# Longer rows in the expert table, first rows zeroed from a batch's own tile, and a new order of work

## The chip, the cores and the metric

The kernel runs on one NeuronCore of a Trainium2 chip. A core has five engines that work through their own instruction streams, each strictly in its written order: TensorE (PE, matrix multiplications; loads of its stationary operand are shown as PEld), VectorE (DVE), ScalarE (ACT), GpSimd (POOL), and SyncE (SP), which here only issues DMAs. They wait for each other, and for DMAs, by semaphores. The metric is the device time of one execution in microseconds. Before the change, three runs took 211.22, 211.44 and 217.73 us; their median is 211.44.

## The reference: what is computed

Two blocks follow each other. The first is an attention with sketched features and no softmax, for 4 batches of 4 heads with 1088 positions of 32 values; the second routes each of the 4352 resulting rows of 128 values to one of 8 experts.

```python
def phi(x):                                   # 8 x 8 products of two sketches
    a = np.einsum('rd,bhsd->bhsr', S1, x)
    b = np.einsum('rd,bhsd->bhsr', S2, x)
    return np.einsum('bhsi,bhsj->bhsij', a, b).reshape(*x.shape[:-1], r * r)
q_p, k_p = (phi(q), phi(k))
kv = np.einsum('bhsf,bhsd->bhfd', k_p, v)
z = np.sum(k_p, axis=2)
num = np.einsum('bhsf,bhfd->bhsd', q_p, kv)
den = np.einsum('bhsf,bhf->bhs', q_p, z)[..., None] + 1e-06
x = (num / den).transpose(0, 2, 1, 3).reshape(B * S, H * D)

logits = x @ w_gate
expert_idx = np.argmax(logits, axis=1)
gate_w = softmax(logits)[np.arange(N), expert_idx]
for e in range(E):
    mask = expert_idx == e
    out[mask] = gate_w[mask, None] * (np.maximum(x[mask] @ w1[e], 0.0) @ w2[e])
```

## The kernel before, in words

The work is cut into named steps, and the string `ORDER` (lines 20 to 49) is the order in which they are recorded. Recording a step appends its instructions to the streams of the engines that it uses; there is no scheduler behind it. So a step that stands early in `ORDER` also stands early in every engine's stream, and whatever waits there holds up all that the same engine has behind it.

**Attention.** `S.t` and `S.m` prepare the sketch matrix; after `S.m` the function `late_constants` (line 287) is called, which builds two constants with copies on GpSimd, `sel` (line 290) and `heads` (line 293). Keys and queries come in chunks of 512 positions: `k21` are the keys of batch 2, chunk 1, `q21` its queries; `kr0` and `kr1` are the 64 positions that are left over of two batches each, `qr0` and `qr1` likewise. Of a chunk, `.t` transposes on PE, `.x` copies to SBUF on ACT, `.a` multiplies by the sketches on PE, `.l`, `.s` and `.o` (ACT, DVE, DVE) form the 64 products, and `.v` of a key chunk sums keys times values on PE. When a batch's keys are done, its steps `e0` to `e3` finish the sums: `.r` adds the remainder, `.k` copies (ACT), `.t` (lines 454 and 460) multiplies by `heads` and `sel` on PE, and `.c`, `.m`, `.z` store the result. Only then can that batch's queries be multiplied (`.n` and `.N`), divided (`.p`, `.e`) and written into `x_rows` (`.y`) and the gate sums (`.g`).

**Routing.** For batch `b`, `rb.a` to `rb.d` choose each row's expert and its place in a table in device memory, `xs_dram`, with 4352 rows for each of 8 experts and one further stretch of the same length. `rb.p` is the part on PE. Then `rb.s0`, `rb.s1` and so on scatter 128 rows each with an indirect DMA from GpSimd (line 641), with `RESTS[b]` small memsets behind each (`breathe`, line 564). A row has `XW` = 130 words: 128 values, the gate weight, and the row's number. The numbers are written into `x_rows` by iotas on GpSimd at the start. Before any row is scattered, the first 128 rows of each of the nine stretches are filled with zeros and a number that is no row's, `ABSENT`, by one DMA on SyncE's queue (line 981); scatters wait for it, since they write the same table.

**Experts.** `t0` to `t2` compute which expert and which rows belong to each tile of 128 rows. Tiles 0 to 9 use rows of batches 0 and 1 alone, later ones those of later batches. Of tile `j7`, `.l` loads the rows (SyncE), `.x` transposes (PE, line 846), `.c` copies, `.w` fetches the first weight (DVE), `.u` and `.U` are the first product (PE, line 863), `.r` and `.q` the rectifier, `.d` the second product (PE, line 898), `.y` scales by the gate weight, and `.s` scatters into the output (GpSimd, line 912). Up to seven further tiles are worked on only when they are needed.

**Loads.** SyncE issues the loads in a fixed order: keys, values and queries of batches 0 to 2, the fill of the table, then batch 3, the remainders of batches 2 and 3, and the experts' weights. A load of batch 3 is issued at the step that gives its buffer back: `do` (line 952) finds that `k00.t` and `k01.t` are both done and issues the keys of batch 3.

Of the kernel before, what the change touches and what calls it, by code (L numbers as in the profile page):

```python
# [10 lines left out]
BF = mybir.dt.bfloat16  # L11
# [6 lines left out]


ORDER = """  # L20
S.t k00.t k00.x S.m k01.t k01.x k00.a kr0.t k00.l kr0.x k00.s k00.o k01.a k01.l kr0.a k01.s k01.o q00.t q00.x
kr0.l q01.t k00.v q00.a k10.t q01.x q01.a k01.v kr0.s kr0.o q00.l q00.s e0.r k11.t k10.x q00.o q01.l q01.s
k10.a q01.o e0.k e0.t e0.m q00.U k11.x k11.a e0.z k10.l k10.s k10.o e0.c q00.d q01.U k11.l q01.T k11.s k11.o
q00.N q00.T q01.d q01.N q01.c q00.p2 q00.e2 q00.y2 q00.c q01.p2 q00.g2 q01.e2 q01.y2 q01.g2 q01.n q01.p q01.e
q01.g q01.y q00.n q00.p qr0.t q11.t q21.t qr0.x qr0.a q20.t q11.x q11.a q20.x q00.e q00.g r0.a r0.x r0.b r0.c
k31.t qr0.l qr0.s q00.y r0.p r0.d r0.s7 r0.s2 r0.s1 r0.s5 r0.s0 r0.s6 r0.s3 r0.s4 k10.v k11.v e1.r k31.x qr0.o
q21.x q21.a q11.l q11.s kr1.t qr0.T e1.k q10.t q21.l q20.a q10.x e1.t q11.o q21.s q20.l q21.o e1.c q11.U e1.m
e1.z q10.a qr0.c q11.d q11.T kr1.x q20.s q20.o q10.l q10.s k30.t q11.c k30.x qr0.n qr0.p k20.t q10.o qr0.e
qr0.y qr0.g q11.N kr1.a q11.p2 q11.e2 kr1.l kr1.s k20.x q11.y2 q11.n q11.p q10.U q10.d k30.a k30.l q11.g2
q10.T q11.e q10.c q11.y k30.s q20.T q10.N k30.o q10.p2 q10.e2 q11.g q10.g2 q10.y2 k21.t k21.x q10.n q10.p  # L30
k20.a q31.t q20.c q10.e q10.g r1.a r1.b q31.x k31.a q21.T r1.x k31.l kr1.o r1.c q30.t q30.x k31.s k21.a q10.y
r1.p q21.c r1.d r1.s6 r1.s2 k20.l k20.s r1.s3 q31.a q20.U qr1.t r1.s8 qr1.x k21.l r1.s0 q20.d k30.v k20.o
q30.a k20.v r1.s1 k21.s k21.o k21.v q31.l k31.o r1.s5 e2.r e2.k qr1.a q31.s q30.l e2.t q31.o e2.m e2.z t0.a
q30.s q30.o k31.v t0.b t0.c e2.c e3.r q21.U e3.k e3.t e3.m q31.U q21.d q20.n q31.d qr1.l q21.n q21.p qr1.s
e3.z q21.e q21.y q21.g q21.N j0.w q20.N q20.p2 qr1.o e3.c q20.p j1.w q20.e q20.y q30.U q30.d q20.g q21.p2
q21.e2 q30.T q30.c q31.T r1.s4 q31.N q21.g2 q20.e2 q31.c q30.N q30.p2 q20.g2 r2.a q30.n r2.b q21.y2 q20.y2
qr1.T q31.p2 q31.e2 q31.g2 q31.y2 q30.p r2.x qr1.c q31.n q31.p q31.e q31.y r1.s7 q31.g q30.e2 q30.g2 r2.p j0.l
j0.x j0.c r2.d j2.w r2.c r2.s5 qr1.n qr1.p j1.l j1.x j0.u j2.l j1.c j0.U j3.l j0.r r2.s2 t0.d j0.q j2.x j2.c
j1.u qr1.e j3.x r2.s3 qr1.g q30.y2 j1.U j2.u j0.d r2.s6 q30.e j4.l j2.U j3.c r2.s4 j3.w j3.u j1.r j2.r r2.s7
j1.q j2.q qr1.y j3.r j4.w j6.l j4.x j4.c t1.a t1.b r2.s0 q30.g r2.s1 r3.a r3.b r3.x t1.c j1.d j2.d j2.y j1.y  # L40
j2.s j1.s t1.d j5.l j3.U j3.q j4.u j5.x j5.c j4.U j4.q j7.l j6.x j6.c j4.r r3.p q30.y j9.l j8.l r3.c j7.x j5.w
j5.u j7.c j5.r j5.U j5.q r3.d r3.s2 r3.s6 j3.d r3.s1 j6.w j6.u j4.d j6.r j3.y j7.w j6.U j11.l j0.y j0.s j8.x
j8.c j9.x j9.c j6.q j7.u j10.l j8.w j4.y r3.s4 j9.w j7.U j12.l j10.w j5.d t2.a t2.b t2.c t2.d j7.q j5.y j7.r
j8.u j8.U j11.w j11.x j9.u j9.U r3.s8 j12.w j5.s j9.q j6.d j6.y j13.l j10.x j10.c j12.x j12.c j7.d j8.q j10.u
j10.U j15.l j11.c j13.w r3.s5 r3.s3 j11.u j10.q j8.r j8.d j12.u j12.U j9.r j9.d j8.y j12.r j10.r j11.U j11.q
j15.x j11.r j13.x j13.c j10.d j15.c j14.l j14.x j17.l j12.q j14.c j13.u j7.y j13.U j3.s j11.d j12.d j16.l
j13.q j13.r j14.w j14.u j14.U j14.r r3.s0 r3.s7 j16.x j15.w j12.y j14.q j15.u j15.r j13.d j16.c j17.x j17.c
j17.w j15.U j14.d
"""
AFTER_LATE = "k11.o"  # L50
PREPARE = (18, 19, 20, 21, 23, 24, 27)
# [3 lines left out]
WARM = 8  # L55
YJ = 12
YREST = 2
RESTS = (3, 1, 3, 3)


@with_exitstack
def kernel(
# [24 lines left out]
    RR = R * R  # L87
    XC = E + D
    KC = XC + 1
    XW = DM + 2  # L90
    HF = F // 2
    JE = -(-(NTOK // 2 - E * 127) // 128)
    JMIN = NTOK // 128
# [14 lines left out]
    def new(name, shape, dtype=FP):  # L108
        return sb.tile(shape, dtype, name=name)
# [14 lines left out]
    def ring(name, n, shape, dtype=FP):  # L124
        return Ring([new(f"{name}{i}", shape, dtype) for i in range(n)])
# [92 lines left out]
    for b in range(B):
        t = new(f"x_rows{b}", [128, J + 1, XW])
        x_rows.append(t)  # L220
        lgh.append(lgh[b - 2] if b > 1 else new(f"lgh{b}", [128, J + 1, H * E]))
        nc.gpsimd.iota(t[:, 0:J, DM + 1].bitcast(I32), pattern=[[1, J]], base=b * S, channel_multiplier=J)
        if b % 2:
            for i in range(2):
                nc.gpsimd.iota(t[i * REM:(i + 1) * REM, J, DM + 1:DM + 2].bitcast(I32), pattern=[[0, 1]],
                               base=(b - 1 + i) * S + MAIN, channel_multiplier=1)
# [81 lines left out]
    kv = {}
# [507 lines left out]
    def expert_tile(j):  # L816
# [3 lines left out]
        @op(x + ".l")  # L820
        def _():
            s["xg"] = xg_bufs.take()
            r = word(tiles[j][1], [SP], E * NTOK)
            d = nc.sync.dma_start(out=s["xg"].bitcast(I32), in_=xs_dram[ds(r, 128), :])
            g = (j >= JE) + (j >= JF)
            if g not in begun:
                begun.add(g)
                for b in range(min(g + 2, B)):
                    for i in scattered[b]:
                        tc.add_manual_dep(d.ins, i.name, landed, reason="rows of the tile")  # L830
            if g < 2:
                tc.declare_no_dep(d.ins, group=f"rows{g}", reason="later rows are in no tile of this group")
                tc.add_to_no_dep_group(f"tiles{g}", d.ins)
# [111 lines left out]
    ends |= {("v", b): {f"k{b}0.v", f"k{b}1.v"} for b in range(B)}  # L945
    weights = list(range(E))

    def tail_loads():
        while weights:
            load_expert(weights.pop(0))  # L950

    def do(name):
        if name[0] == "r" and name[1] in "23":
            assert name[:1] + str(int(name[1]) - 2) + name[2:] in done or name[2:4] == ".s"
        if name[0] == "q" and name[1] in "23" and name[3:5] == ".g" or name == "qr1.g":
            assert f"r{1 if name == 'qr1.g' else int(name[1]) - 2}.a" in done
        if name in ("r2.d", "r3.d"):
            assert f"t{int(name[1]) - 2}.a" in done
        ops.pop(name)()
        done.add(name)  # L960
        for m, es in list(ends.items()):
            if name in es and es <= done:
                del ends[m]
                wide.give(main[m].rearrange("p h j d -> p (h j d)"))
                if waiting:
                    n, src, b = waiting.pop(0)
                    load_main(nc.sync, n, src, b)
                    if not waiting:
# [12 lines left out]
    nc.sync.dma_start(out=xs_dram.rearrange("(e n) w -> n e w", n=NTOK)[0:128], in_=fill[:, None, :].bitcast(I32).broadcast_to([128, E + 1, XW]))
# [98 lines left out]
```

## Time and profile before

| | |
|---|---|
| median of the runs | 211.44 us |
| the profiled execution, its own time | 213.85 us |
| its span, first to last instruction | 212.1 us |
| mean granted PE clock | 0.988 |
| PE busy | 201.0 us, 95% |
| DVE, POOL, ACT busy | 120.2, 108.8, 80.2 us |
| DMA packets, bytes | 29279, 23.32 MB |
| scatters into the table (line 641) | 34, mean 1.10 us of POOL |
| scatters into the output (line 912) | 41, about 1.0 us of POOL each |

The page divides the span into 40 slices of 5.3 us and gives each engine's busy share in tenths. The list of waits says for an engine's line which instruction or DMA ended the idle time before it: total, times, longest. The timeline has one row for each instruction or run of equal ones: start, duration, engine and line, what it writes and reads, and in brackets how long its engine had been idle and what released it. `SPq` rows are DMA issues. PE's durations overlap, since matmuls are pipelined.

### The profile page before, as it was taken

The numbers are of one execution on the slowest core, as the hardware profiler recorded it, in microseconds if no ns is written. First come the engines' busy times: TensorE is split into PE (matmuls) and PEld (weight loads), VectorE is DVE, ScalarE is ACT, GpSimd is POOL, SyncE is SP. The second block draws the span as 40 slices with busy tenths as digits, with TensorE's granted clock in tenths as the row PEclk, the third lists the DMA queues.
The fourth block names the chain that finished last, engine by engine and source line by source line (L and its number), as shares of the span: only waits on it lengthen the run. The fifth ranks groups of instructions, "written<-read, shape, count | busy, mean of one in ns | idle before, by whom it ended". The sixth has DMA issues, their size and how long they took to land. (4 is left out here: it accounts for less than half of the span.)

```text
span 212.1 us, 6120 instructions
## 1 busy us (share of the span) xinstructions
PE 201.0 (95%) x2107; PEld 196.7 (93%) x2107; DVE 120.2 (57%) x381; ACT 80.2 (38%) x218; POOL 108.8 (51%) x211
## 2 busy tenths in 40 slices
PE   7999779999997999999999999999998999999991
PEld 7899769998896999999999999999997999999991
DVE  4598877889988886988303342535335423241410
ACT  2457337573442343542432143242332333223220
POOL 6100038757980477867766777777430355036033
PEclk9999999999998899999999999999999999999998
DMA  5999979999712311021011102223310120001000
GB/s 141 295 317 275 237 186 302 380 381 374 256 39 66 81 37 33 20 77 50 28 44 49 39 28 57 68 65 101 95 40 22 36 47 26 0 17 34 17 23 16
DMA packets 29279, 23.32 MB, mean 110 GB/s; under 512 B 5866, under 2 KB 27116, under 8 KB 29248
## 3 DMA queue, kind: packets, MB, share of 16 engines
q1 hardware_dynamic: 26304, 18.15, 30.7%
q0 software_dynamic: 2400, 4.50, 6.4%
q8 instruction: 19, 0.31, 0.6%
q10 hardware_dynamic: 544, 0.26, 0.4%
q14 instruction: 12, 0.10, 0.2%
HBM read 17.81 MB, written 5.55 MB: 110 GB/s over the span
## 5 line engine op out<-in xcount | busy, mean ns | idle before, releaser
L863 PE MATMUL bank<-xgT,wide 128*128 128x128 f32 x592 | 73.2, 277 | 0.0
L863 PEld LDWEIGHTS bank<-xgT,wide 128*128 128x128 f32 x592 | 70.4, 195 | 0.0
L641 POOL DMA_INDIRECT xs_dram<-x_rows,row_i x34 | 37.4, 1099 | 45.6 <-DMA q_rem<-in_q_dram 23.0
L889 DVE TENSOR_SCALAR hTb<-bank 128x512 f32<-128x512 f32 x27 | 18.6, 691 | 64.5 <-PE bank L863 44.9
L912 POOL DMA_INDIRECT out_dram<-y,to x23 | 22.8, 992 | 39.3 <-ACT xgT L851 21.0
L898 PE MATMUL bank<-w_all,hTa 128*128 x296 | 39.3, 276 | 1.0 <-DVEq L1010 1.0
L898 PE MATMUL bank<-w_all,hTb 128*128 x296 | 39.2, 275 | 0.0
L898 PEld LDWEIGHTS bank<-w_all,hTa 128*128 128x128 f32 x296 | 36.0, 192 | 1.2 <-issue 1.1
L898 PEld LDWEIGHTS bank<-w_all,hTb 128*128 128x128 f32 x296 | 36.0, 192 | 0.0
L907 ACT ACTIVATE y<-bank,xg 128x128 f32<-128x128 f32 x37 | 13.1, 369 | 55.2 <-PE bank L898 53.2
L880 ACT ACTIVATE hTa<-bank 128x512 f32<-128x512 f32 x37 | 21.9, 600 | 23.5 <-PE bank L863 19.9
L858 DVE COPY wide<-w_all 128x1024 f32 x39 | 27.8, 730 | 2.5 <-issue 2.3
L566 POOL MEMSET fill<- 1x130 f32 x108 | 26.3, 243 | 3.6
L912 POOL DMA_INDIRECT out_dram<-y,xg x18 | 18.5, 1027 | 9.3 <-issue 5.2
L395 DVE TENSOR_TENSOR wide<-sum 128x1024 f32<-128x1024 f32 (+1 forms) x18 | 20.3, 1135 | 0.6
L366 PE MATMUL bank<-s_cat,xT 128*128 128x128 f32 x136 | 19.0, 280 | 0.0
L366 PEld LDWEIGHTS bank<-s_cat,xT 128*128 128x128 f32 x136 | 16.7, 192 | 0.4 <-ACT xT L359 0.2
L522 PE MATMUL bank<-kvx,q_pT 128*128 128x82 f32 x128 | 15.4, 272 | 0.0
L522 PEld LDWEIGHTS bank<-kvx,q_pT 128*128 128x128 f32 x128 | 15.0, 192 | 0.0
L359 ACT COPY xT<-bank 128x512 f32<-128x512 f32 (+1 forms) x20 | 10.3, 525 | 10.6 <-PE bank L354 10.4
L851 ACT COPY xgT<-bank 128x128 f32<-128x128 f32 x41 | 10.0, 265 | 8.0 <-PE bank L846 7.7
L354 PE MATMUL bank<-ident,wide 128*128 128x128 f32 x64 | 9.6, 281 | 2.4 <-DMA wide<-in_k_dram 2.4
(156 smaller groups left out, 180.1 us busy)
## 6 DMA issues: line engine op xcount, KB each, us to landing
w_all<-in_moe_w_dram SPq DMA_DIRECT2D x16, 512.0 KB, 6.3
xg<-xs_dram SPq DMA_DIRECT2D x41, 65.0 KB, 1.9
wide<-in_v_dram SPq DMA_DIRECT2D x4, 512.0 KB
wide<-in_q_dram SPq DMA_DIRECT2D x4, 512.0 KB, 11.2
wide<-in_k_dram SPq DMA_DIRECT2D x3, 512.0 KB
xs_dram<-fill SPq DMA_DIRECT2D x1, 585.0 KB
xs_dram<-x_rows,row_i POOLq DMA_INDIRECT x34, 2.8
out_dram<-y,to POOLq DMA_INDIRECT x23, 2.2
```

Of the source, the lines that this page charges most:

```text
L366: nc.tensor.matmul(t[:, ts(i, 128)], lhsT=st["xT"][:, ts(i, 128)], rhs=s_cat.rearrange("p w t g r -> p (w t g r)"), start=True, stop=True)
L395: nc.vector.tensor_tensor(dst, a[:, :, :, None].broadcast_to([128, n * 4, R, R]), b[:, :, None, :].broadcast_to([128, n * 4, R, R]), ALU.mult)
L522: nc.tensor.matmul(o, lhsT=lhsT, rhs=kvx[b][:, hp].rearrange("p g c -> p (g c)"), start=True, stop=True)
L566: nc.gpsimd.memset(fill[0:1], 0.0)
L641: d = nc.gpsimd.indirect_dma_start(out=xs_dram[:], out_offset=bass.IndirectOffsetOnAxis(ap=st["row"][:, u:u + 1], axis=0), in_=x_rows[b][: ...
L858: nc.vector.tensor_copy(out=s["w1"], in_=w1_all[:, ds(r, F)])
L863: nc.tensor.matmul(t[:, ts(c, 128)], lhsT=s["w1"][:, ts(c0 + c, 128)], rhs=s["xT"], start=True, stop=True)
L880: nc.scalar.activation(s["hTa"], s["ha"], AF.Relu)
L889: nc.vector.tensor_scalar(s["hTb"], s["hb"], 0.0, None, ALU.max)
L898: nc.tensor.matmul(t[:, :DM], lhsT=h[:, ts(c % 4, 128)], rhs=w2_all[:, ds(r + c * DM, DM)], start=(c == 0), stop=(c == 7))
L907: nc.scalar.activation(s["y"], s["py"][:, :DM], AF.Copy, bias=0.0, scale=s["xg"][:, DM:DM + 1])
L912: d = nc.gpsimd.indirect_dma_start(out=out[:], out_offset=bass.IndirectOffsetOnAxis(ap=s["to"](), axis=0), in_=s["y"], in_offset=None, bou ...
```

## The change

- A row of the table has 144 words (576 bytes) instead of 130 (520). The tiles still load 130 words of each. Words 130 to 143 of `x_rows` are set to zero at the start, on GpSimd for batches 0 to 2, on DVE for batch 3.
- The fill no longer comes from a tile of its own. The tile `x_rows` of batch 3 (`last_rows`) is zeroed on DVE at the start, and given `ABSENT` as number by one iota; its first columns also serve as `zeros` for the warming matmuls. `fill_rows` writes eight rows of it, 4,608 bytes in one piece, to eight rows of the table: 128 partitions to 8 experts times 16 pieces, and 16 partitions to the ninth stretch. Then `number_rows(3)` writes the true numbers of batch 3 into the tile, with three iotas on GpSimd.
- `fill_rows` is called from `do`, right behind the load of the keys of batch 3. So on SyncE's queue these keys come first and the fill, now two DMAs, second.
- The constants `upper`, `base_e` and `tri`, made by ten DVE instructions in `later_constants` behind `k11.o`, are made on GpSimd at the start.
- No rest is left behind the scatters of batch 1 (`RESTS`).
- `ORDER` is another order of the same steps throughout; more steps of the last tiles stand in it. Only its first lines are shown.

```diff
 ORDER = """
-S.t k00.t k00.x S.m k01.t k01.x k00.a kr0.t k00.l kr0.x k00.s k00.o k01.a k01.l kr0.a k01.s k01.o q00.t q00.x
-kr0.l q01.t k00.v q00.a k10.t q01.x q01.a k01.v kr0.s kr0.o q00.l q00.s e0.r k11.t k10.x q00.o q01.l q01.s
-k10.a q01.o e0.k e0.t e0.m q00.U k11.x k11.a e0.z k10.l k10.s k10.o e0.c q00.d q01.U k11.l q01.T k11.s k11.o
...
+S.t k00.t k00.x k01.t S.m k00.a k01.x k00.l k00.s kr0.t k00.o k01.a kr0.x kr0.a q01.t k01.l k01.s k01.o q00.t
+k00.v q00.x kr0.l kr0.s kr0.o k11.t k11.x q00.a q00.l q00.s q00.o k01.v e0.r e0.k q01.x k11.a k11.l e0.t e0.m
+e0.c k11.s k11.o e0.z q10.t q10.x q01.a q01.l q11.t q11.x q01.s q01.o q00.T q00.c q10.a q10.l q00.U q11.a
...
-RESTS = (3, 1, 3, 3)
+RESTS = (3, 0, 3, 3)
...
-    XW = DM + 2
+    XW = DM + 16
...
-    zeros = new("zeros", [128, 128])
+    last_rows = new("x_rows3", [128, J + 1, XW])
+    zeros = last_rows[:, 0, 0:128]
     nc.vector.memset(zeros, 0.0)
+    nc.vector.memset(last_rows[:, 1:J], 0.0)
+    nc.vector.memset(last_rows[:, 0, 128:XW], 0.0)
+    nc.vector.memset(last_rows[:, J, DM:XW], 0.0)
...
+    nc.gpsimd.iota(last_rows[:, 0:J, DM + 1].bitcast(I32), pattern=[[0, J]], base=ABSENT, channel_multiplier=0)
...
+    def number_rows(b):
+        t = x_rows[b]
         nc.gpsimd.iota(t[:, 0:J, DM + 1].bitcast(I32), pattern=[[1, J]], base=b * S, channel_multiplier=J)
         if b % 2:
             for i in range(2):
                 nc.gpsimd.iota(t[i * REM:(i + 1) * REM, J, DM + 1:DM + 2].bitcast(I32), pattern=[[0, 1]],
                                base=(b - 1 + i) * S + MAIN, channel_multiplier=1)
 
+    for b in range(B):
+        t = last_rows if b == B - 1 else new(f"x_rows{b}", [128, J + b % 2, XW])
+        if b < B - 1:
+            nc.gpsimd.memset(t[:, :, DM + 2:XW], 0.0)
...
+        if b < B - 1:
+            number_rows(b)
+
+    upper = new("upper", [128, 128], BF)
+    nc.gpsimd.affine_select(out=upper, in_=ones_b, compare_op=ALU.is_gt, fill=0.0, base=0, pattern=[[1, 128]],
+                            channel_multiplier=-1)
+    base_e = new("base_e", [128, E])
+    iota(base_e, [[NTOK, E]])
+    tri = new("tri", [128, E, E])
+    nc.gpsimd.memset(tri, 1.0)
+    nc.gpsimd.affine_select(out=tri, in_=tri, compare_op=ALU.is_ge, fill=0.0, base=0, pattern=[[1, E], [-1, E]],
+                            channel_multiplier=0)
...
-    def later_constants():
-        nc.vector.tensor_scalar(upper, col, iota_p, None, ALU.is_gt)
-        nc.vector.tensor_copy(out=base_e, in_=ebase)
-        for e in range(E):
-            nc.vector.tensor_scalar(tri[:, e, :], rev, float(E - e) - 0.5, None, ALU.is_ge)
...
-            d = nc.sync.dma_start(out=s["xg"].bitcast(I32), in_=xs_dram[ds(r, 128), :])
+            d = nc.sync.dma_start(out=s["xg"].bitcast(I32), in_=xs_dram[ds(r, 128), 0:DM + 2])
...
+    def fill_rows():
+        rows8 = last_rows[:, 0:J].rearrange("p j w -> p (j w)").bitcast(I32)
+        x4 = xs_dram.rearrange("(e n) w -> e n w", n=NTOK)
+        nc.sync.dma_start(out=x4[0:E, 0:128].rearrange("e (c j) w -> e c (j w)", j=J), in_=rows8)
+        nc.sync.dma_start(out=x4[E, 0:128].rearrange("(c j) w -> c (j w)", j=J), in_=rows8[0:128 // J])
+        number_rows(B - 1)
...
                     load_main(nc.sync, n, src, b)
+                    if n == "k":
+                        fill_rows()
...
-    nc.sync.dma_start(out=xs_dram.rearrange("(e n) w -> n e w", n=NTOK)[0:128], in_=fill[:, None, :].bitcast(I32).broadcast_to([128, E + 1, XW]))
```

More of the change, by code (lines that the diff above doesn't have):

```diff
@@ L20 @@
 ORDER = """
-S.t k00.t k00.x S.m k01.t k01.x k00.a kr0.t k00.l kr0.x k00.s k00.o k01.a k01.l kr0.a k01.s k01.o q00.t q00.x
-kr0.l q01.t k00.v q00.a k10.t q01.x q01.a k01.v kr0.s kr0.o q00.l q00.s e0.r k11.t k10.x q00.o q01.l q01.s
-k10.a q01.o e0.k e0.t e0.m q00.U k11.x k11.a e0.z k10.l k10.s k10.o e0.c q00.d q01.U k11.l q01.T k11.s k11.o
-q00.N q00.T q01.d q01.N q01.c q00.p2 q00.e2 q00.y2 q00.c q01.p2 q00.g2 q01.e2 q01.y2 q01.g2 q01.n q01.p q01.e
-q01.g q01.y q00.n q00.p qr0.t q11.t q21.t qr0.x qr0.a q20.t q11.x q11.a q20.x q00.e q00.g r0.a r0.x r0.b r0.c
@@ L26 @@
[L26 to L45, printed above, removed]
@@ L46 @@
-j15.x j11.r j13.x j13.c j10.d j15.c j14.l j14.x j17.l j12.q j14.c j13.u j7.y j13.U j3.s j11.d j12.d j16.l
-j13.q j13.r j14.w j14.u j14.U j14.r r3.s0 r3.s7 j16.x j15.w j12.y j14.q j15.u j15.r j13.d j16.c j17.x j17.c
-j17.w j15.U j14.d
+S.t k00.t k00.x k01.t S.m k00.a k01.x k00.l k00.s kr0.t k00.o k01.a kr0.x kr0.a q01.t k01.l k01.s k01.o q00.t
+k00.v q00.x kr0.l kr0.s kr0.o k11.t k11.x q00.a q00.l q00.s q00.o k01.v e0.r e0.k q01.x k11.a k11.l e0.t e0.m
+e0.c k11.s k11.o e0.z q10.t q10.x q01.a q01.l q11.t q11.x q01.s q01.o q00.T q00.c q10.a q10.l q00.U q11.a
@@ new lines @@
+q10.s q10.o q00.d q11.l k10.t q01.U q01.d q00.N q11.s q11.o q00.p2 q00.e2 q00.g2 q00.y2 q01.T q01.c q00.n
+q00.p q00.e q00.y q01.N q00.g q01.p2 qr0.t q01.n qr0.x q11.U q01.e2 q01.y2 q01.p qr0.a q01.g2 k10.x q01.e
+qr0.l q01.g q11.d q21.t q11.T q11.c r0.a k20.t k20.x r0.b r0.x q20.t qr0.s q01.y r0.c k10.a qr0.o r0.p q10.T
+k10.l r0.d k21.t r0.s1 r0.s5 r0.s6 r0.s2 r0.s7 q20.x q20.a r0.s4 k10.s q20.l k10.o q10.U k20.a q20.s q20.o
+q10.c q21.x k20.l k20.s q30.t k10.v r0.s3 k11.v e1.r e1.k q21.a e1.t k20.o e1.m e1.z k21.x q21.l q21.s qr1.t
@@ new lines @@
+qr0.T e1.c q10.d q21.o k21.a k21.l k21.s k21.o q11.N qr1.x q11.p2 q11.e2 qr0.c kr1.t kr1.x q11.n q11.p q11.e
+q10.N q10.p2 q11.g q11.y q11.g2 q10.e2 q30.x q10.g2 q10.n q10.y2 q10.p q10.e qr0.n r0.s0 q10.y qr0.p q20.U
+k30.t kr1.a k20.v k30.x k21.v q31.t qr0.e qr1.a q10.g qr0.g kr1.l q20.d r1.a r1.b qr0.y kr1.s kr1.o q31.x r1.x
+q11.y2 k30.a k30.l r1.c r1.p r1.d r1.s3 r1.s8 r1.s7 r1.s6 r1.s2 r1.s4 r1.s0 k31.t k31.x k30.s q21.T e2.r t0.a
+e2.k q20.T q21.U t0.b e2.t qr1.l q21.d e2.m e2.z qr1.s qr1.o q31.a q30.a k31.a e2.c k30.o q21.c q20.N q21.n
@@ new lines @@
+t0.c q20.c q20.n r1.s1 r1.s5 j0.l qr1.T q30.l q30.s q30.o j1.w k31.l q21.p q21.N q21.p2 q30.U k31.s k31.o
+q31.l q20.p2 q31.s q31.o k30.v k31.v e3.r qr1.c q30.T q20.e2 q20.g2 e3.k q20.p j1.l q30.d e3.t e3.c q20.y2
+e3.m e3.z j4.l q31.T q31.c q21.e q31.U q31.d q30.N q30.c q21.e2 q21.y2 q30.p2 q31.n qr1.n qr1.p q31.p q30.n
+q20.e q20.y q20.g q21.g q21.g2 q30.p r2.a r2.b r2.x q21.y q31.N j0.x j0.c j0.w q30.e q30.y q30.g r2.p r2.d
+r2.c r2.s5 r2.s2 r2.s1 r2.s6 r2.s0 r2.s4 r2.s7 q31.e j1.x j1.c j0.u j0.U r2.s3 j3.w j0.r j0.q q30.e2 qr1.e
@@ new lines @@
+j1.u q30.y2 q30.g2 j2.l j2.x j1.r t0.d j2.w j1.U j3.l q31.p2 j5.l qr1.y q31.e2 j0.d j3.x j1.q j2.c j1.d qr1.g
+j4.x q31.y j3.c j4.c j1.y j1.s j2.u j2.U j7.l j2.q j3.u j3.r j3.U j5.x q31.g2 j5.c q31.y2 q31.g j4.w j4.u j4.r
+r3.a j2.r j4.U r3.b j6.l j8.l j5.w j0.y j5.u j5.U j3.q j6.x j4.q t1.a j9.l j6.c j6.w r3.p r3.d j2.d t1.b t1.c
+j5.r j5.q j3.d j7.w j6.u j6.U j9.w r3.x j2.y t1.d r3.c j9.x j2.s j6.r r3.s5 j7.x r3.s2 j7.c r3.s1 j11.l j4.d
+t2.a j8.x j0.s j8.c j4.y j9.c j6.q j7.u j7.U j7.r j5.d j5.y j10.l j7.q j8.w j8.u j4.s j12.l j9.u j9.U j14.l
@@ new lines @@
+t2.b j8.U j9.r r3.s7 j11.w j10.x j10.c j10.w j5.s j6.d j6.y j6.s j7.d j8.r j8.q j10.u j10.r j11.x j11.c j12.x
+j9.q j8.d r3.s4 j7.y t2.c j11.u j11.U j9.d j10.U j13.l j13.x j8.y r3.s8 j11.r j12.w j12.c j12.u j15.l j12.U
+j17.l j13.c j11.q j13.w j13.u j14.w j13.U j12.r j3.y j14.x r3.s0 j14.c j10.q j3.s j12.q j10.d j10.y j15.x
+j13.q j14.u j14.U j16.w j16.l j16.x j15.w t2.d j16.c j11.d r3.s6 j15.c j15.u j15.r j15.U j15.q j18.w r3.s3
+j13.r j12.d j12.y j16.u j16.U j14.q j18.l j19.l j17.x j13.d j14.r j17.c j17.w j14.d
@@ L133 @@
     kvz_bufs = ring("kvz", 2, [128, 96])
-    xg_bufs = ring("xg", 13, [128, XW])
+    xg_bufs = ring("xg", 13, [128, DM + 2])
     xgT_bufs = ring("xgT", 7, [128, 128])
@@ L203 @@
     iota(iota_p, [[0, 1]], per_partition=1)
-    col = new("col", [128, 128])
-    iota(col, [[1, 128]])
     ones_b = new("ones_b", [128, 128], BF)
@@ L213 @@
     iota(jio, [[1, NI]])
-    fill = new("fill", [128, XW])
-    nc.gpsimd.memset(fill, 0.0)
-    nc.gpsimd.iota(fill[:, DM + 1:DM + 2].bitcast(I32), pattern=[[0, 1]], base=ABSENT, channel_multiplier=0)
+    fill = new("fill", [1, XW])
+    nc.gpsimd.iota(last_rows[:, 0:J, DM + 1].bitcast(I32), pattern=[[0, J]], base=ABSENT, channel_multiplier=0)
     x_rows, lgh = [], []
[L218 to L221, printed above, removed]
+    def number_rows(b):
+        t = x_rows[b]
         nc.gpsimd.iota(t[:, 0:J, DM + 1].bitcast(I32), pattern=[[1, J]], base=b * S, channel_multiplier=J)
@@ L226 @@
                                base=(b - 1 + i) * S + MAIN, channel_multiplier=1)
+    for b in range(B):
+        t = last_rows if b == B - 1 else new(f"x_rows{b}", [128, J + b % 2, XW])
+        if b < B - 1:
+            nc.gpsimd.memset(t[:, :, DM + 2:XW], 0.0)
+        x_rows.append(t)
+        lgh.append(lgh[b - 2] if b > 1 else new(f"lgh{b}", [128, J + 1, H * E]))
+        if b < B - 1:
[9 more added lines that the diff above has]
+                            channel_multiplier=0)
     def warm(n):
@@ L282 @@
     heads = new("heads", [128, 2, NP, XC])
-    upper = new("upper", [128, 128], BF)
-    base_e = new("base_e", [128, E])
-    tri = new("tri", [128, E, E])
     def late_constants():
@@ L977, in after @@
             late_constants()
-        if name == AFTER_LATE:
-            later_constants()
-    nc.sync.dma_start(out=xs_dram.rearrange("(e n) w -> n e w", n=NTOK)[0:128], in_=fill[:, None, :].bitcast(I32).broadcast_to([128, E + 1, XW]))
     for name in ORDER.split():
```

## The prediction

> **What bounds the kernel now.** I read the page first. TensorE (PE) is busy almost everywhere, so a microsecond that PE loses is a microsecond of the span, if nothing gives it back.
>
> ```profile
> span 212.1 us, 6120 instructions
> ...
> PE   7999779999997999999999999999998999999991
> ...
> PEclk9999999999998899999999999999999999999998
> ```
>
> Each digit is a fortieth, 5.3 us: PE's dips are at the start, at 21 to 32 us, near 64 to 69 us and at the end. Two rows of the list of waits name those in between:
>
> ```profile
> PE bank L354 <- DMA wide<-in_k_dram: 2.4, 1, 2.4
> PE bank L620 <- DVE oh L606: 1.2, 1, 1.2
> ```
>
> The first is `k31.t` at 27.7 us, waiting for the keys of batch 3; the second is `r2.p` at 66.5 us. The windows put the stages side by side (stretch, length, then busy us and count for PE, PEld, DVE, ACT, POOL, then granted PE clock, DMA share, GB/s):
>
> ```profile
> 15.00:18.00 3.00, 3.00 (x36) 2.86 (x35) 2.34 (x6) 1.99 (x5) 0.00 (x0) 1.00 1.08 349
> ...
> 20.00:22.00 2.00, 2.00 (x21) 2.00 (x20) 1.90 (x14) 0.83 (x3) 0.00 (x0) 1.00 1.28 105
> 22.00:24.00 2.00, 2.00 (x21) 2.00 (x20) 1.38 (x8) 1.07 (x4) 0.00 (x0) 1.00 1.20 190
> ...
> 15.96:67.00 51.04, 46.66 (x688) 44.47 (x688) 43.29 (x140) 25.68 (x77) 26.45 (x50) 1.00 0.86 256
> ...
> 67.00:70.50 3.50, 3.49 (x21) 3.10 (x22) 2.93 (x14) 0.86 (x4) 0.00 (x0) 0.51 0.36 81
> 70.50:187.00 116.50, 115.55 (x1043) 115.37 (x1042) 58.68 (x189) 40.67 (x109) 68.46 (x123) 1.00 0.17 46
> ```
>
> DMA runs at 349 GB/s, falls to 105 while the zero rows are written, and recovers. The expert tiles, from 67 us on, leave PE no gaps: what is lost before them is not won back in them. The last views are the timelines of SyncE, GpSimd (POOL) and PE around the moved fill.
>
> ```profile
> 11.73 1.77 SPq L156 DMA_DIRECT2D wide<-in_q_dram  x1
> 13.61 0.88 SPq L981 DMA_DIRECT2D xs_dram<-fill  x1
> 14.54 3.51 SPq L156 DMA_DIRECT2D wide<-in_k_dram  x1
> ```
>
> ```profile
> 3.60 0.24 POOL L222 IOTA x_rows<- 128x8 int32 x2
> 3.77 0.33 POOL L225 IOTA x_rows<- 64x1 int32 x2
> ...
> 6.02 0.40 POOL L290 COPY sel<-m 128x256 f32<-128x256 f32 x1 [1.91 <-DVE m L289]
> ...
> 6.36 0.29 POOL L293 COPY heads<-ident 128x128 f32<-128x128 f32 x1
> ...
> 15.96 0.36 PE L454 MATMUL bank<-heads,kvz 128*64 128x80 f32 x4
> ```
>
> POOL finishes `sel` and `heads` at 6.65 us, and `e0.t` (PE, L454), which multiplies by both, comes at 15.96.
>
> **The change, step by step.** The step that decides is a wait that is not in the diff's words. `fill_rows` issues its two DMAs and then calls `number_rows(3)`: three iotas on POOL that overwrite words which those DMAs read, so they wait until both have landed. It runs inside `k01.t`. In the new order `S.m` stands behind `k01.t` (before: ahead of it), and `S.m` brings the POOL copies of `sel` and `heads`. So on POOL, which runs in order, those two copies now stand behind iotas that wait for the fill; and PE, in order too, stops at `e0.t`.
>
> *When does the fill land?* Up to 18.0 us the windows moved 4.73 MB (129, 300 and 308 GB/s for 5 us each, 349 for 3). Ahead of the fill stood nine loads of 512 KB and six of 32 KB, 4.92 MB, so the rest is through at 18.6. Now the keys of batch 3 go first: 524 KB at 349 GB/s, 1.5 us, 20.1. The fill has grown to 1152 rows of 576 bytes, 664 KB. Fast end: 349 GB/s, 1.9 us. Slow end: before, 599 KB took from about 18 to 24 us, so 664 KB takes 6.7. To landing I add 1.5 us (a load of 65 KB in the page takes 1.9 from issue to landing, with its transfer). That gives 23.5 to 28.3 us. The pieces of 4,608 bytes resemble the weight loads, the direction resembles the old fill; I take 25.5. [...]
>
> *From there to `e0.t`:* three iotas take 0.50 us (3.60 to 4.10), `sel` and `heads` 0.63 (6.02 to 6.65), hand-over 0.1: 26.7 us. PE itself would be there at about 14.7 (15.96 before, less the work below), so it stands for 12 us.
>
> *Sum, as a shift of the first expert tile (`j0.x`, 67.0 us before):*
> - `e0.t` starts at 26.7 instead of 15.96: +10.7.
> - `q01.a` and `k10.t`, ahead of `e0.t` before, stand behind it now. A pass of 128 columns takes 0.112 us (16 in 1.79 in the chain); `q01.a` is 8, `k10.t` 4: +1.3. All else ahead of `j0.x` is the same work (`qr1.n` comes in, `r2.p` goes out, half a microsecond each).
> - Of the 51.0 us from `e0.t` to `j0.x` my count of the passes (0.11 each at 128 columns, 0.62 for a chunk's key sums, 0.35 to 0.5 for the small products of a batch) explains 45.3; of the other 5.7 some go: 2.35 for `k31.t` (its load is now ahead of the fill, and long landed), 0.4 at the remainder keys, 1.2 at `r2.p` (now behind `j0.x`), 0.15 at the tile itself: -4.1. Late after that are the small hand-overs among PE, DVE and ACT, 1.6 us, which stay.
> - Half clock: PE ran at 0.51 from 67.0 to 70.4, right after the idle 1.35 us, 1.7 us lost; without the idle time: -1.7.
> - The long stand costs a half clock of its own. At the start, after idle time, 16 warming passes took 3.79 us, twice the price, until about 5.6 us: 4.5 us at half speed, +2.2.
>
> Sum +8.4. [...]
>
> *The scatter chain asks for the same.* From `e0.t` to `r0.p` there are 13.2 us of passes: 26.7 + 13.2 + 2.2 + 0.5 of waits = 42.6, first scatter 1.5 later as before (28.1 to 29.7): 44.1. Eight with three rests at 2.23 (38.52 to 40.75): 62.0. Nine without rests at 1.28 (the output scatters at 142.37 and 143.65): 73.5. From the last scatter's end to `j0.x` it was 4.0 (63.05 to 67.0): 77.5. PE's own count gives 67.0 + 8.4 + 1.7 = 77.1. The later one counts: **+8.8**. The removed rests are worth 0.07 each here.
>
> *Cost nothing:* zeroing `last_rows` on DVE at the start (1,040 words, 0.3 to 1.2 us between the 0.17 of 128 words and a copy of 1024 at 0.73) falls into DVE's idle 0.98 us ahead of the sketches, and what sticks out vanishes in the stand. Moving `upper`, `base_e` and `tri` from DVE (1.0 us at 20.4) to POOL's start: PE is the bound there, POOL idle. Tile loads still read 520 bytes; scattered rows grow by a tenth, with 2.8 us to landing, inside the 4.0 above. The loads behind the fill are needed after 45 us, the weights were in by 57.
>
> Profiled time: 213.85 around a span of 212.1, so 222.6 around 220.9. The runs shown have their median 2.4 lower, 211.44; from there **220.2**.
>
> **Rivals.**
> - *The fill is in time* (7%). If the fill landed before PE comes to `e0.t`, by about 13.5 us, the stand and its half clock fall out and the credits remain: -4.1 - 1.7, about 206. For it: both credits are in the views above, and any landing ahead of that point frees the copies. Against: it is issued after 14 us behind 5.4 MB.
> - *The fill overtakes the loads* (7%): engines serving it beside the loads land it near 21; the shift shrinks by 4.5, to about 215.5. Against: the old one, issued at 13.6, only starts to weigh on the rate at 18.
> - *The fill writes slowly* (16%): at half the engines and at the old pace, 31 us or more; +5.5, about 225.7. For it: 105 GB/s at 20 to 22 us.
> - *My forecast* (70%), 217 to 223.5 by the landing's two ends, the half clock coming back at `j0.x` (+1.7) included.
>
> Range 215 to 226.5: it leaves the first rival out and the far end of the third. A measurement of this kernel tells about 2% from no change: faster (under 207.2) 0.06, within 0.08, slower (over 215.7) 0.86.
>
> **What would show it.** POOL idle from about 5 to 25 us, released by the fill's DMA at an iota; PE idle 10 to 12 us at the matmul from `heads`; a half clock behind it; `k31.t` without a wait; first scatter near 44, first tile near 77; equal spacing of tiles from there. It is wrong if the copies of `sel` and `heads` run at 6 us, or if the fill lands far from 25.5: each microsecond there is one of the result.

## The result, and the profile after

The changed kernel takes 224.57 us (median of 4 runs, 223.67 to 226.14), the kernel before 211.83 (4 runs beside it); the ratio is 1.062, 95% interval 1.054 to 1.070. On a second chip it was 222.79 and 1.052 (1.047 to 1.057). Forecast: 220.2, range 215.0 to 226.5, slower. The mechanism is the predicted one; the size was 4.4 us short. (Some executions of the kernel before and of its relatives lie some 2 to 3% higher at a granted clock of about 0.97; the ratios leave them out, the medians do not.)

First the page of the kernel after: span, TensorE (PE) and its granted clock in 40 slices, each now 5.6 us.

```profile
span 223.3 us, 6102 instructions
...
PE   7960599999998799999999999999999899999992
...
PEclk9995579999999969999999999999999999999998
```

The fourth slice is empty: PE does nothing at all from 16.7 to 22.3 us. The clock is at half around it, and again in one slice near 80 us. The rest of the row is as full as before. The list of waits for PE names the hole:

```profile
PE bank L462 <- POOL heads L308: 10.3, 1, 10.3
PE bank L854 <- DMA xg<-xs_dram: 1.2, 1, 1.2
...
PE bank L412 <- DVE wide L403: 0.5, 1, 0.5
PE bank L854 <- DVE rk L637: 0.3, 1, 0.3
```

10.3 us at line 462, which is `e0.t`, for `heads`. The waits of the kernel before for the keys of batch 3 (2.4), for the remainder keys (0.4) and at `r2.p` (1.2) are gone from the list. In their place stands the first expert tile (line 854, `j0.x`), which waits for its rows. The timeline of GpSimd (POOL) shows why `heads` is late:

```profile
4.29 0.29 POOL L244 TENSOR_SCALAR_AFFINE_SELECT tri<-tri 128x64 f32<-128x64 f32 x1
23.77 0.15 POOL L222 IOTA x_rows<- 128x8 int32 x1 [19.19 <-DMA xs_dram<-x_rows]
23.87 0.32 POOL L225 IOTA x_rows<- 64x1 int32 x2
24.25 0.40 POOL L305 COPY sel<-m 128x256 f32<-128x256 f32 x1
24.59 0.29 POOL L308 COPY heads<-ident 128x128 f32<-128x128 f32 x1
42.88 1.15 POOL L649 DMA_INDIRECT xs_dram<-x_rows,row_i  x1 [18.00 <-DVE row_i L643]
```

The iota in the second row stood 19.19 us for the fill's DMA. The two copies wait for nothing of their own; they are only behind it. On PE:

```profile
13.84 0.83 PE L374 MATMUL bank<-s_cat,xT 128*128 128x128 f32 x6
24.93 0.54 PE L462 MATMUL bank<-heads,kvz 128*64 128x80 f32 x4 [10.27 <-POOL heads L308]
...
75.32 1.50 PE L530 MATMUL bank<-kvx,q_pT 128*128 128x82 f32 x12
77.98 0.30 PE L854 MATMUL bank<-ident,xg 128*128 128x128 f32 x1 [1.15 <-DMA xg<-xs_dram]
```

`e0.t` starts at 24.93 instead of 15.96, and `j0.x` at 77.98 instead of 67.01; its row in the timeline of the kernel before is this one:

```profile
67.01 0.44 PE L846 MATMUL bank<-ident,xg 128*128 128x128 f32 x1 [0.15 <-DMA xg<-xs_dram]
```

That is 10.97 of the 11.2 us by which the span grew. The windows of the kernel after (stretch, length, busy us and count for PE, PEld, DVE, ACT, POOL, granted clock, DMA share, GB/s) add what happens after the stand and at the first tile:

```profile
20.00:22.00 2.00, 0.00 (x0) 0.00 (x0) 0.00 (x0) 0.00 (x0) 0.00 (x0) 0.50 1.05 404
22.00:24.00 2.00, 0.00 (x0) 0.00 (x0) 0.00 (x0) 0.00 (x0) 0.22 (x2) 0.50 0.95 296
...
24.93:30.95 6.02, 6.02 (x37) 5.99 (x38) 3.62 (x7) 2.58 (x6) 0.00 (x0) 0.50 0.89 244
30.95:77.98 47.03, 44.85 (x664) 42.53 (x663) 41.46 (x127) 23.49 (x72) 23.40 (x41) 1.00 0.54 184
78.70:82.20 3.50, 3.37 (x16) 3.40 (x17) 3.04 (x17) 0.86 (x2) 1.58 (x4) 0.51 0.38 97
```

PE works 6.02 us at half clock after the stand (3.0 us lost) and another 3.4 at the first tile (1.7 lost, just as in the profile of before). And the DMA rate no longer falls while the zero rows are written: 404 and 296 GB/s, where it was 105 and 190. That is what the longer rows bring (`e6` below), and here it comes while PE stands still.

So from `e0.t` to `j0.x` there are now 53.05 us, 51.04 before. Of those, 3.0 are half clock and 1.33 are `q01.a` and `k10.t`, which stood ahead of `e0.t` before (the prediction's estimate). The remainder, 48.7, is 2.3 less than before.

### The profile page after: what moved, and what is told of

The parts are those of the page before. It is cut to its first block, busy times and chain, and to the rows that moved or that the text cites. A ratio compares the mean times of both kernels' runs of the same rounds, so it can differ in the third digit from the quotient of the medians.

```text
span 223.3 us, 6102 instructions
## 1 busy us (share of the span) xinstructions
PE 204.1 (91%) x2107; PEld 200.2 (90%) x2107; DVE 120.3 (54%) x374; ACT 80.2 (36%) x218; POOL 106.0 (47%) x207
## 5 line engine op out<-in xcount | busy, mean ns | idle before, releaser
L649 POOL DMA_INDIRECT xs_dram<-x_rows,row_i x34 | 35.9, 1056 | 39.7 <-DVE row_i L643 18.0
L574 POOL MEMSET fill<- 1x144 f32 x99 | 23.9, 241 | 3.6
L920 POOL DMA_INDIRECT out_dram<-y,xg x18 | 18.6, 1033 | 8.2 <-issue 6.1
L374 PEld LDWEIGHTS bank<-s_cat,xT 128*128 128x128 f32 x136 | 17.8, 205 | 0.1
L854 PE MATMUL bank<-ident,xg 128*128 128x128 f32 x41 | 10.1, 278 | 1.5 <-DMA xg<-xs_dram 1.2
```

The lines of the kernel that those rows point to most:

```text
L374: nc.tensor.matmul(t[:, ts(i, 128)], lhsT=st["xT"][:, ts(i, 128)], rhs=s_cat.rearrange("p w t g r -> p (w t g r)"), start=True, stop=True)
L574: nc.gpsimd.memset(fill[0:1], 0.0)
L649: d = nc.gpsimd.indirect_dma_start(out=xs_dram[:], out_offset=bass.IndirectOffsetOnAxis(ap=st["row"][:, u:u + 1], axis=0), in_=x_rows[b][: ...
L920: d = nc.gpsimd.indirect_dma_start(out=out[:], out_offset=bass.IndirectOffsetOnAxis(ap=s["to"](), axis=0), in_=s["y"], in_offset=None, bou ...
```

## The experiments

**Theory:** the whole loss is GpSimd's order. The copies of `sel` and `heads` stand behind iotas that wait for the fill. **Rivals:** the new order of work, the removed rests or the longer rows cost time by themselves; the fill's shape (8 outermost pieces) makes the wait long. The first job (the four kernels from `e1` to `e4`) ran on a chip where the kernel before took 230.5 us (227.7 to 233.4). No profile of it was taken there, so these four are compared with each other. The second job ran where the kernel before took 212.37, the third where it took 211.66.

**e1, the copies first.** One word of `ORDER` moves; the rest of the order stays new.

```diff
-S.t k00.t k00.x k01.t S.m k00.a k01.x k00.l k00.s kr0.t k00.o k01.a kr0.x kr0.a q01.t k01.l k01.s k01.o q00.t
+S.t k00.t k00.x S.m k01.t k00.a k01.x k00.l k00.s kr0.t k00.o k01.a kr0.x kr0.a q01.t k01.l k01.s k01.o q00.t
```

> The changed kernel with one word of the order moved: S.m ahead of k01.t, so that on GpSimd the copies of sel and heads stand ahead of the three iotas that wait for the fill. Every other engine's instructions stay in their places. Theory (the copies behind the iotas are the whole loss): sel and heads are done by about 7 us, the matmul from heads starts near 14.7 us instead of 24.9, nothing runs at half clock behind it. Of the profiled span of 223.3 us go 10.2 for the stand and 3.0 for the half clock of 6 us behind it: 210 us; 208 if the half clock at 78.7 us goes too. Rival (the new order, or the longer rows and the later fill, cost by themselves): the stand goes, but the span stays above 215 us.

Measured: 215.69 us (214.87 to 216.72). The stand is gone and with it the half clock (mean granted clock 1.0). On the same chip `e2`, which keeps the stand, took 228.34, 12.65 us more; it differs from `e1` in the shape of the fill too, but that left the landing where it was. The profiled span, 213.2, lies between the two expectations (210, and above 215): PE waits 1.3 us for the rows of the first tile, and 2.1 us at line 412 and 1.2 at line 906 for nothing that the trace shows. The comparison with the kernel before (0.945, 0.934 to 0.955) says little, since that one was itself slow on this chip; hence the repetition below.

**e2, the fill on 16 engines.** The outermost dimension of the large piece becomes 16.

```diff
-        nc.sync.dma_start(out=x4[0:E, 0:128].rearrange("e (c j) w -> e c (j w)", j=J), in_=rows8)
+        nc.sync.dma_start(out=x4[0:E, 0:128].rearrange("e (c j) w -> c e (j w)", j=J), in_=rows8)
```

> The changed kernel with the pieces of the fill outermost in its destination (16 pieces, then 8 experts) instead of the experts; the same bytes go to the same rows. Theory (a leading dimension of 8 keeps the large piece on 8 of the 16 DMA engines): all 16 engines work on it, the fill lands near 22.2 us instead of 23.6, and the stand at heads, and with it the whole, is 1.4 us shorter: span 222. Rival (the writes themselves set the pace): it lands at 23.6 as before and the span stays at 223.3.

Measured: 228.34 us (227.15 to 229.83). The trace marks when each DMA engine has done its part. In the changed kernel, the large piece has one step at 15.50 and eight marks from 22.70 to 23.41, where the loads around it have sixteen: by the marks, eight engines served it. With 16, fifteen marks lie between 21.68 and 22.44, and one at 23.51. The bulk is a microsecond earlier, the last mark is not: one engine lags by 1.1 us in this DMA, and by 1.0 to 1.3 in the four loads around it. The small piece, behind it, ends at 23.71, against 23.64 in the changed kernel and 23.58 in `e4`, which has the old shape on the same chip; GpSimd's rows say the same (the timeline of `e2`):

```profile
23.84 0.15 POOL L222 IOTA x_rows<- 128x8 int32 x1 [19.25 <-DMA xs_dram<-x_rows]
```

So the engine count is seen, but 16 engines didn't land the fill sooner: there the slowest engine set the end. With eight, it seems to have had no part in the large piece: of the small piece's marks in `e4`, seven lie at 20.17 to 20.51 and one 1.6 us behind them, at 22.13, and only then come eight, from 23.05 to 23.58, that stood behind the large piece. The changed kernel itself was not run on this chip, so this comparison is one of landings and not of times.

**e3, warming matmuls in the stand.** 44 warming calls (88 matmuls) stand behind `k11.a`, where PE would idle. They compute nothing of the output.

```diff
+        if name == "k11.a":
+            warm(44)
```

> The changed kernel with 44 more warming matmuls on zeros (88 passes, 9.8 us at full clock) on TensorE right behind k11.a, where it would stand until 24.9 us. Theory (the stand costs a half clock of its own): the clock stays whole from 25 to 31 us, the first expert tile comes 3.0 us sooner, span 220.3. Rival (behind the stand other engines, or the scatter chain, set the pace): the clock stays whole, but the span falls by less than 1 us.

Measured: 224.31 us (223.30 to 225.21), 4.0 less than `e2` on the same chip. Page and timeline of `e3`:

```profile
PEclk9999999999999999999999999999999999999998
```

```profile
14.59 9.99 PE L250 MATMUL bank<-x_rows 128*128 128x128 f32 x88
26.07 0.36 PE L462 MATMUL bank<-heads,kvz 128*64 128x80 f32 x4 [1.49 <-POOL heads L308]
```

The clock is whole until the last microseconds, though `e0.t` starts 1.1 us later than in `e2` because the fill landed later. From `e0.t` to `j0.x` it took 51.4 us, against 54.8 in `e2`: 3.4 less, of which 1.6 are `e2`'s wait for the tile's rows and 1.7 its half clock. At the first tile `e2` has one more half clock, of 3.41 us (1.7 lost), and `e3` has none; with the later start of 1.1 us these add up to the 4.0. The stretch from `e0.t` to the first scatter, which has the same work in all runs with the new order and the stand, measures the half clock by itself:

| kernel | half clock after `e0.t`, us | lost (half of it) | `e0.t` to first scatter |
|---|---|---|---|
| e3 | 0 | 0 | 15.12 |
| e2 | 3.45 | 1.7 | 16.70 |
| e4 | 4.49 | 2.2 | 17.23 |
| c_after (below) | 5.04 | 2.5 | 17.49 |
| after | 6.02 | 3.0 | 17.95 |

The last column follows the third within 0.2 us. In these runs the half clock behind the stand is a cost of its own, of 1.7 to 3.0 us.

**e4, no rests behind the scatters of batch 0.**

```diff
-RESTS = (3, 0, 3, 3)
+RESTS = (0, 0, 3, 3)
```

> The changed kernel without the three memsets behind each of the eight scatters of batch 0. Theory (the scatter chain and TensorE's own work reach the first expert tile together, the chain by 1.15 us the later): the eight scatters take 1.3 us each instead of 2.25, the rows of the first tile are there 7 us sooner, the wait of 1.15 us at 78 us goes, and the half clock behind it (1.7 us) if the idle time brought it: span 222.1 or 220.4. Rival (the rests matter to nothing, or the denser scatters get in the way of the loads of weights): no change, or slower.

Measured: 241.89 us (240.69 to 242.85), 13.6 more than `e2`. The scatters come mostly every 1.28 us as meant, from 42.10 on, but PE no longer runs its small matmuls in one piece (timeline of PE in `e4`):

```profile
46.37 0.33 PE L412 MATMUL bank<-wide,wide 128*32 128x64 f32 x5 [0.42 <-issue]
47.10 0.34 PE L412 MATMUL bank<-wide,wide 128*32 128x64 f32 x5 [0.40 <-issue]
47.86 0.32 PE L412 MATMUL bank<-wide,wide 128*32 128x64 f32 x5 [0.42 <-issue]
48.59 0.33 PE L412 MATMUL bank<-wide,wide 128*32 128x64 f32 x5 [0.41 <-issue]
```

Five matmuls every 0.72 us; "issue" means that neither another engine nor a DMA was being waited for. The expected gain did not come. PE's waits put down to issue come to 9.2 us in `e4`, against 2.8 in `e2`, and two half clocks of 10.24 us each (from 49.84 and from 77.15 on) stand where `e2` has one of 3.41: by estimate 6.4 and 8.5 us more, which is the size of the loss. I took dense scatters, beside the weights' loads, for the cause; `e8` and `e10` below test that for batch 1, and there it falls. For batch 0 it stays open, since on this chip `e1`, `e2` and `e3`, with the rests of batch 0 in place, had such idle places too (2.1, 1.7 and 1.7 us at line 412).

**c_after and c_before, both kernels again** on the second chip, unchanged.

> The changed kernel once more, beside the others of this job and the kernel before on the same chip, so that edits are compared within one chip. All theories: the matmul from heads near 25 us, its idle time near 10 us, slower than the kernel with the copies first by about 10 us or more.

> The kernel before once more, with a profile, since the kernel before took 228 to 233 us on the chip of the first job against 211 to 218 in the runs shown. If that chip feeds TensorE its instructions more slowly while GpSimd scatters, the profile shows idle time of TensorE that nothing in it explains, at the many small matmuls of the key sums; if the slow clock did it, the same idle places at a lower granted clock; if this is another chip, a span near 212 us as shown.

Measured: 222.79 for the changed kernel (222.46 to 224.45), the stand 10.3 us, `e0.t` at 25.11, the first tile at 77.67; and 214.0 for the kernel before (211.48 to 217.63), ratio 0.998 (0.995 to 1.001). Two executions of the second, 211.48 and 211.83, had a granted clock of 1.0. The profiled one, 217.63, has an idle place of 1.7 us at line 404, put down to issue, and a half clock of 13.65 us from 55.33 on. Nothing near 230 us came up on this chip, so what made the first one slow stays open.

**e5, the changed kernel under the old order.** Everything in the change but its `ORDER`: long rows, fill behind the keys, number rows, no rests in batch 1. In the old order `S.m` stands ahead of `k01.t`.

> The changed kernel with the order of the kernel before; rows of 144 words, the fill in pieces behind the keys of batch 3, constants on GpSimd and no rests for batch 1 stay. In the old order S.m stands ahead of k01.t, so the copies stand ahead of the waiting iotas. Theory (the place of the copies is the loss, the other parts are gains): no stand; the wait of 2.4 us for the keys of batch 3 and 0.4 us at their remainders are gone; 2 to 3 us below the kernel before on the same chip, and within 3 us of the changed kernel with the copies first. Rival (the longer rows, the later fill or the missing rests cost by themselves): as slow as the kernel before or slower.

Measured: 210.94 us, ratio 0.993 (0.989 to 0.998), beside 222.79 for the change with its own order. The list of waits of `e5` for PE, past the start:

```profile
PE bank L412 <- issue: 1.1, 1, 1.1
PE bank L906 <- DVEq L1024: 0.9, 1, 0.9
PE bank L628 <- DVE oh L614: 0.6, 1, 0.6
```

No stand, and no wait for keys or for the tile's rows. Without the new order the change costs nothing, so the loss needs that order; the rest of the change makes the kernel about 0.7% faster, 1.4 us, less than the 2 to 3 us expected.

**e6, the long rows alone** in the kernel before, its fill still issued ahead of the keys.

```diff
-    XW = DM + 2
+    XW = DM + 16
...
-    xg_bufs = ring("xg", 13, [128, XW])
+    xg_bufs = ring("xg", 13, [128, DM + 2])
...
-        t = new(f"x_rows{b}", [128, J + 1, XW])
+        t = new(f"x_rows{b}", [128, J + b % 2, XW])
+        nc.gpsimd.memset(t[:, :, DM + 2:XW], 0.0)
...
-            d = nc.sync.dma_start(out=s["xg"].bitcast(I32), in_=xs_dram[ds(r, 128), :])
+            d = nc.sync.dma_start(out=s["xg"].bitcast(I32), in_=xs_dram[ds(r, 128), 0:DM + 2])
```

(A second table, `lgh`, gets the same smaller shape, which makes room.)

> The kernel before with nothing changed but the rows: 144 words (576 bytes), of which the tiles still load 130; the fill is still 1152 pieces, now of 576 bytes, ahead of the keys of batch 3. [...] Rival (many small pieces are slow whatever their length): the rate still falls, no change in time.

Measured: ratio 0.994 (0.991 to 0.998), a gain of 1.2 us. Windows of `e6`:

```profile
20.00:22.00 2.00, 2.00 (x20) 2.00 (x20) 1.90 (x15) 0.87 (x3) 0.00 (x0) 1.00 1.13 354
22.00:24.00 2.00, 2.00 (x20) 2.00 (x20) 1.38 (x8) 1.02 (x4) 0.00 (x0) 1.00 1.07 347
```

354 and 347 GB/s against 105 and 190 in the kernel before, with the same number of rows and the same place in the queue. The longer rows alone take the slow stretch away, and the wait of 2.4 us for the keys of batch 3 with it; the rival falls. Moving the fill behind the keys adds nothing that can be told from this (0.993 and 0.994).

**e7 to e10: what is the new order worth without the stand, and what do the rests do?** Four kernels beside each other on the third chip: copies first (`e1` again), the same with three rests behind each scatter of batch 1, the old order (`e5` again), and that with the rests.

```diff
-RESTS = (3, 0, 3, 3)
+RESTS = (3, 3, 3, 3)
```

> The changed kernel with one word moved in its order: S.m ahead of k01.t, so that GpSimd's copies of sel and heads are done at 6 us and nothing stands behind the waiting iotas. Repeated where the other three kernels of this job run beside it, since the chip of its first run had the kernel before at 230. If the stand was the whole loss and the new order is otherwise as good as the old one: 210 to 212 with the kernel before at 212, and within 0.5% of the changed kernel under the old order. If the new order has a cost of its own (its first scatters come no earlier, more of its queries stand behind them, no rests in batch 1 beside loads): 213 to 216 and 1% or more behind the old order.

> As the kernel with the copies first, but three rests behind each scatter of batch 1 instead of none. If dense scatters are what starves TensorE near 52 us (2.1 us of PE idle ahead of the sketch products of 32 columns, put down to issue, in the first run of that kernel): those idle places fall under 0.8 us and the time falls by 1 to 2 us against the kernel without rests. If the scatters of batch 1 are on the chain to the first expert tile instead: the last scatter comes about 9 us later, the wait for the first tile grows, and the time rises by 2 us or more.

> The changed kernel under the order of the kernel before, again, as the partner of the others: 210.9 with the kernel before at 212.4, ratio 0.993 as on the first chip.

> As the changed kernel under the old order, with three rests behind each scatter of batch 1 instead of none. If dense scatters starve TensorE: the 1.1 us of idle PE at the sketch products near 52 us go, 209.5 to 210.5. If the chain of scatters sets the first tile: nine scatters at 2.25 instead of 1.28 end about 9 us later, the wait for the first tile grows from 0.2 us to some microseconds, 213 or more.

| kernel | median, us | ratio to before (95%) | first scatter | `j0.x` | PE's wait there |
|---|---|---|---|---|---|
| e7, copies first | 212.48 | 1.003 (0.997 to 1.008) | 29.68 | 65.41 | 1.7 |
| e8, copies first, rests | 218.82 | 1.034 (1.030 to 1.038) | 29.92 | 71.99 | 8.0 |
| e9, old order | 211.92 | 0.992 (0.986 to 0.998) | 27.57 | 64.13 | none |
| e10, old order, rests | 218.48 | 1.032 (1.027 to 1.036) | 27.57 | 70.78 | 6.2 |

With one word moved the change costs nothing that can be measured, where it cost 5 to 6%. POOL's timeline of `e7`:

```profile
5.99 0.40 POOL L305 COPY sel<-m 128x256 f32<-128x256 f32 x1 [1.41 <-DVE m L304]
6.33 0.29 POOL L308 COPY heads<-ident 128x128 f32<-128x128 f32 x1
25.04 0.15 POOL L222 IOTA x_rows<- 128x8 int32 x1 [18.42 <-DMA xs_dram<-x_rows]
25.13 0.30 POOL L225 IOTA x_rows<- 64x1 int32 x2
29.68 1.16 POOL L649 DMA_INDIRECT xs_dram<-x_rows,row_i  x1 [4.25 <-DVE row_i L643]
```

The iota still waits 18 us, but nothing that PE needs soon stands behind it. What is left against the old order, 1.1% by the ratios (their intervals just touch), is more than the 0.5% expected if the stand was all. It has a visible place: the first scatter comes 2.1 us later, PE waits at the first tile, and a half clock comes with it. That this is the cause is read from one profile of each kernel and not tested. The page's clock rows of `e7` and then of `e9`:

```profile
PEclk9999999999996799999999999999999999999999
```

```profile
PEclk9999999999999999999999999999999999999999
```

The rests tell the two theories of those expectations apart. Three rests stretch a scatter of batch 1 from 1.28 to 2.25 us; its nine scatters end 6.5 us (`e8`) and 7.3 us (`e10`) later, and PE waits for the tile (lists of waits of `e8` and `e10`):

```profile
PE bank L854 <- DMA xg<-xs_dram: 8.0, 1, 8.0
```

```profile
PE bank L854 <- DMA xg<-xs_dram: 6.2, 1, 6.2
PE bank L412 <- issue: 1.2, 1, 1.2
```

Made longer like this, the chain of scatters sets the first tile. And the idle place at line 412 is still there with the rests (1.2 us in `e10`, 0.8 in `e9`), and absent without them in `e7`: that the scatters of batch 1 stand close together does not cause it. That guess falls.

## Why the prediction was right, point by point

- **The stand: right.** The step that decides was the wait that the diff doesn't name, and `e1`, `e5` and `e7` take it away by order alone. PE stood 10.3 us.
- **When the fill lands: 25.5 taken, 23.64 measured** (23.5 to 28.3 were the ends). I had split the difference between the fast row (349 GB/s) and the old fill's pace. `e6` shows that the old pace belonged to rows of 520 bytes; the new rows go at the fast end. `e0.t` was therefore at 24.93 and not 26.7: 9.0 us instead of 10.7 for the largest term.
- **Half of the engines for the large piece: right, and no reason for a late landing.** Only the third rival took it, and no run ahead of the prediction shows it for a DMA of this shape. The marks of `after` do: eight, from 22.70 to 23.41, where the loads around it have sixteen. The fill was in at 23.64 all the same, and in `e2` 16 engines landed it no sooner (23.71), since one of them lagged by 1.1 us.
- **Half clock after the stand: 2.2 taken, 3.0 measured** in the profiled run (6.02 us at 0.50), 1.7 to 2.5 in three others (3.45 us in `e2`, 4.49 in `e4`, 5.04 in `c_after`); `e3` takes it away.
- **Credits of 4.1 for stalls that go: they went, but 2.3 was left at the first tile.** The keys of batch 3, the remainder keys and `r2.p` left the list of waits. In their place came 1.15 at the tile's rows, and ahead of it 0.5 at line 412 and 0.3 at line 530.
- **The half clock at 67 us, -1.7: wrong.** This is the step that failed. It rested on "without the idle time", while my own second count had the scatters' chain at 77.5 and PE at 77.1, that is PE idle just there. It idled 1.15 us, and the half clock came back (0.50 from 78.73 to 82.15). The range allowed for it; the forecast didn't.
- **And it was counted twice.** I took 1.7 off for a half clock seen in the profiled execution, and then 2.4 because that execution lies above the median of its runs. But the half clock is at least part of those 2.4: seven executions of the kernel before on the second chip, at 211.5 to 212.5 us, have a granted clock of 0.995 to 1.0, the profiled one at 213.85 has 0.988. What a profiled run has and the median run has not must not be credited in both places. The miss of 4.4 us is then: 1.7 for the half clock, 2.0 for the offset (2.4 taken; the profiled execution of the kernel after, 224.99, lies 0.4 above its median), 0.5 for the first tile (77.5 against 77.98), 0.2 for the rest.
- **The scatters' chain asks for the same: right to 0.5 us, by two errors that offset each other.** First scatter 42.88 instead of 44.1, 1.2 early; the ninth then comes 18.6 us later (17.9 taken), and the last one ends 12.5 after that (11.5 taken), with single scatters at 1.9 and 1.3 us. That the errors nearly cancel is luck. `e8` and `e10` show that this chain, not PE's own count, is what decides when it is lengthened.
- **Rests at 0.07: right for the one rest removed** (spacing 1.34 to 1.28), but not a price per rest: three cost 0.97 per scatter, and by the ratios 6.6 us of the time in `e8` (against `e7`) and 8.4 in `e10` (against `e9`).
- **Costs taken as nothing: right.** PE's first wait for zeros is 1.1 us before and after; GpSimd's new constants end at 4.58, before `sel` could start (its input came at about 5.9).
- **The first rival ("the fill is in time", 206) had the wrong price.** `e7` frees the copies as that rival would, and gives 1.003, not 206. The wait for the keys was worth less than its 2.35: without it (`e6`) the kernel gains 0.6%, 1.2 us, and another idle place, 1.6 us at line 405, appears. And the new order starts its scatters later.
- **The range held partly by luck.** The 224.57 lies above my own band (217 to 223.5), in the room that the range kept for a fill that writes slowly (225.7). That rival is false: the fill landed 1.9 us early. By the prediction's own rule, a microsecond of the landing is one of the result; with the landing at the 25.5 taken, the same other errors would have made about 226.4, an estimate, at the very end of the range.

What stays open: why PE idles at times at the small matmuls (line 412; line 404 and 405 before), so also what set off the 13.6 us of `e4`, and why one chip ran the kernel before at 230. In these places the trace names no engine or DMA that PE waited for.

## What to carry to other kernels

On an engine that works in order, look at what stands *behind* a new wait: here three iotas that nobody needed soon held two copies that PE needed at once, and one word in the order was worth 5 to 6%. A stall that goes is a credit only up to the next chain that asks for the same time, and a half clock or any other accident of the profiled execution may be missing from the median run; take it off once. Where rows are written by DMA, try their length on its own before moving the transfer.

## What the runs showed of the hardware that I had not expected

- Rows of 520 bytes written to DRAM held the whole DMA traffic at 105 and 190 GB/s in two windows of 2 us (`before`, 20 to 24 us); rows of 576 bytes, otherwise alike, ran at 354 and 347 (`e6`). Which property of the rows makes the difference, these runs don't show.
- Leaving out those that a run ends in, the half clocks of these traces lasted 3.41 us at the first tile of the kernel before and after, of `c_after` and `e2`, 6.83 in `e7` and `e8`, 10.24 in `e10` and twice more in `e4`, 13.65 in `c_before`, and 10.24 (`e2`, `e4`) or 13.65 (after, `c_after`) around the stand. At the first tile one came with an idle time of 1.1 to 1.7 us (before, after, `c_after`, `e2`, `e7`) and of 6.2 and 8.0 (`e10`, `e8`), and none with 0.2 to 1.1, `r2.p` included (`e3`, `e5`, `e6`, `e9`), or with 1.3 in `e1`. So a bit more than a microsecond of idle time went with a half clock in some runs and not in others.
- One DMA engine is 1.0 to 1.3 us behind the others in load after load of `e2`, so there the fill over 16 engines landed no earlier (23.71) than over 8 in `e4` (23.58).
- The fill's wait ended at 23.7 to 23.9 where PE stood idle (`after`, `c_after`, `e2`, `e4`), and at 24.5 to 25.3 where PE worked (`e1`, `e3`, `e5`, `e7` to `e10`), warming matmuls included. The marks show what was late: in these seven, one or two of the eight engines finish the large piece 0.7 to 1.4 us after the rest, whose last mark, 23.1 to 23.6, is where the early runs have theirs. Whether PE's work has to do with it, no run here tells.
